# Seventeen small extra loads queued behind the first V load of a single-token attention and ReGLU block

## The chip, the cores and the metric

One Trainium2 chip, one core of it. The metric is the device time of one execution in microseconds (us). The kernel before was timed three times: 1038.66 us in the median, 1038.58 to 1039.75 us in all.

## The reference, cut to what matters

One token goes through an attention block with a long cache and then through a gated feed-forward block, everything in float32:

```
q   = layernorm(x) @ wq                     # 640 -> 32 heads x 192
s   = q . k_cache * 192 ** -0.5             # 8192 keys a head
o   = softmax(s) . v_cache
h   = x + concat(o) @ wo
out = h + (relu(n @ W_gate) * (n @ W_up)) @ W_down    # n = layernorm(h), 640 -> 1536 -> 640
```

The caches hold 32 heads x 8192 positions x 192 numbers each, 201 MB for K and as much for V. Each number is read once and used once, for a single token.

## The kernel before, in words

Everything the core reads is packed on the host into long rows, one row for each of the 128 partitions of SBUF, so that a load is always a block of 128 partitions. For head h, `kk[h]` is the K block (12288 float32 a row, 6144 KB in all) and `vv[h]` the V block (14208 a row, 7104 KB: the V cache of the head, its slice of `wo`, and the `wq` of the next head). The last V block comes from `v0` in two pieces, the `wq` of the first head with the input x from `w0`, and the feed-forward weights lie in `ww`, loaded in six pieces that `CUTS` sets. All of them go into one SBUF tile, `big`: one place for K and two places for V, in turn.

SyncE (SP) issues all of these loads, in the order of its program (`sync_fn`): `w0`, K of head 0, V of head 0, and then a loop over two heads at a time that issues K, V, K, V. K of head i waits for the semaphore `sp`, which TensorE raises when the scores of head i - 1 are done (line 132), since there is a single place for K. V of head i waits for `wo`, raised when the output of an earlier head has been multiplied with its slice of `wo` (line 137). Behind the loop come the last K in two halves, the last V in two pieces, and, after the last scores and outputs (lines 155 and 156), the six pieces of `ww` (line 158). Line 160 stores the result.

For each head TensorE makes the query (`query`, out of the `wq` that came with the V block before), the scores (`scores`, 24 matmuls into the PSUM tile `sp`), and the output (`output`). VectorE takes the maxima and multiplies V with the weights of the softmax (`ttr`, line 126, 12 of them a head, with `columns` in the middle). ScalarE makes the exponentials and the masks. TensorE's matmuls all have line 328, that of a helper. The feed-forward block at the end takes each piece of `ww` as it lands (`weights`, line 399, and `project`): its last matmuls into `pq` need the last two pieces.

GpSimd (POOL) fills constants at the start. At the end it waits for the result (`s_o4`, line 185) and clears the semaphores (line 186). A small load of x (four rows of 160 numbers, line 288) goes out on ScalarE's queue at the start. It is the only load on that queue.

Words used below: a "packet" is one piece of a load that one of the core's 16 DMA engines moves. A "closing write" is the four-byte packet with which an engine reports the end of its part of a load to the load's semaphore; a load raises its semaphore by 16 in all. A "landing" is the moment at which all of a load has been reported.

Of the kernel before, what the change touches and what calls it, by code (L numbers as in the profile page):

```python
# [10 lines left out]
P, Q, NQ = 128, 32, 4  # L11
# [15 lines left out]
JV = 7  # L27
GATE, DOWN, FW = DJ * F, 2 * DJ * F, 2 * DJ * F + FJ * D
CUTS = (0, GATE, GATE + 3 * F, DOWN + 2 * D, DOWN + 8 * D, DOWN + 11 * D, FW)
SCALE = DH ** -0.5  # L30
EPS = 1e-5

# [26 lines left out]
def mha_decode_reglu_kernel(nc, x, w0, kk, vv, v0, ww, out):  # L59
    names = ("xr", "k", "k2", "va", "vb", "vb1", "qd", "qs", "sp", "mp", "pt", "m1", "rs",  # L60
             "pl", "q", "op", "po", "o", "o2", "wo", "cst", "st", "ffn0", "ffn1", "ffn2", "ffn3", "ffn4",
             "ffn5", "h4", "hm", "hc", "hr", "pu", "us", "pg", "gu", "pd", "pool", "dve")
    stored, s_o4 = (nc.alloc_semaphore("e_" + n) for n in ("out", "o4"))
    s = {n: nc.alloc_semaphore("e_" + n) for n in names}
    nums = sorted(x.num for x in s.values())
# [2 lines left out]
    def sb(name, shape):  # L68
        return nc.alloc_sbuf_tensor(name, shape, F32).ap()

    def ps(name, shape):
        return nc.alloc_psum_tensor(name, shape, F32).ap()
# [33 lines left out]
    h4 = sb("h4", [P, DG])  # L106
    hs1 = sb("hs1", [P, 1])
    hT = sb("hT", [P, DJ, Q])
    hc = sb("hc", [P, DJ, Q])
    hsq = sb("hsq", [P, DJ])  # L110
    us = sb("us", [P, FG])
    gu = sb("gu", [P, FG])
    guT = sb("guT", [P, FJ, Q])
    o4 = sb("o4", [P, DG])

    sp = ps("sp", [P, SG])
    pq = ps("pq", [P, QB])
# [7 lines left out]
    def ttr(eng, dst, a, b, scale, res):  # L125
        return eng.tensor_tensor_reduce(out=res, in0=a, in1=b, scale=scale, scalar=0.0,  # L126
                                        op0=ALU.mult, op1=ALU.add, accum_out=dst)

    def sync_fn(sy):
        def load_k(h, n, dst=kt, c=slice(0, KW), sem="k"):  # L130
            if n is not None:
                sy.wait_ge(s["sp"], n)
            sy.dma_start(dst[:, c], kk[h][:, c]).then_inc(s[sem], 16)  # L133

        def load_v(h, n, b):
            if n is not None:
                sy.wait_ge(s["wo"], n)
            sy.dma_start(vts[b], vv[h]).then_inc(s["vb" if b else "va"], 16)

        sy.dma_start(vt2[:, VW + KW + WO:2 * VW + DJ], w0).then_inc(s["vb"], 16)  # L140
        load_k(0, None)
        load_v(0, None, 0)
        sy.sem_inc(s["k2"], 16 * (H - 1))
        sy.sem_inc(s["vb1"], 16 * (H // 2))
        with sy.Fori(1, H - 2, 2) as i:
            load_k(i, i)
            load_v(i, i, 1)
            load_k(i + 1, i + 1)
            load_v(i + 1, i + 1, 0)
        load_k(H - 1, H - 1, c=slice(0, KW // 2))  # L150
        load_k(H - 1, None, c=slice(KW // 2, KW), sem="k2")
        sy.wait_ge(s["wo"], H - 1)
        for c0, c1, n in ((0, JV * SG, "vb"), (JV * SG, KW + WO, "vb1")):
            sy.dma_start(vts[1][:, c0:c1], v0[:, c0:c1]).then_inc(s[n], 16)
        sy.wait_ge(s["wo"], H)
        sy.wait_ge(s["sp"], H)
        for i, (c0, c1) in enumerate(zip(CUTS, CUTS[1:])):
            sy.dma_start(big[:, c0:c1], ww[:, c0:c1]).then_inc(s[f"ffn{i}"], 16)  # L158
        sy.wait_ge(s_o4, 1)
        sy.dma_start(out[0].rearrange("o (g n) -> (o g) n", g=NQ), o4[0:P:Q, :]).then_inc(stored, 16)  # L160

    def pool_fn(g):
        c = Chain(g, s["pool"])
        c(g.memset(ones, 1.0))
        c(g.memset(share, 1.0 / C))
        c(g.memset(eps, EPS))
        c(g.memset(pick, 0.0))
        c(g.memset(op, 0.0))
        c(g.memset(rl, 1.0))
        c(g.memset(vts[1][:, KW:KW + WO], 0.0))  # L170
        c(g.memset(ident, 0.0))
        c(g.memset(quad, 1.0))
        c.sync()
        c(g.affine_select(out=quad, in_=quad, compare_op=ALU.is_ge, fill=0.0, base=0,
                          pattern=[[1, P]], channel_multiplier=-Q))
        c(g.affine_select(out=ident, in_=ident, compare_op=ALU.not_equal, fill=1.0, base=0,
                          pattern=[[-1, P]], channel_multiplier=1))
        for i in range(2):
            c(g.memset(pick[:, i, i, :], 1.0))
        c.sync()  # L180
        c(g.affine_select(out=quad, in_=quad, compare_op=ALU.is_ge, fill=0.0, base=Q - 1,
                          pattern=[[-1, P]], channel_multiplier=Q))
        c.sync()
        g.sem_inc(s["cst"], 1)
        g.wait_ge(s_o4, 1)
        g.sem_clear(range(nums[0], nums[-1] + 1))

    def vector_fn(v):
# [42 lines left out]
        def columns(n):  # L231
            v.wait_ge(s["q"], n)
            ttr(v, q[:, 0:1], ident, pq[:, 0:D1], SCALE, junk[:, 0:D1])
            ttr(v, q[:, 1:2], low, pq[:, D1:DH], SCALE, junk[:, D1:DH]).then_inc(s["qd"])

# [90 lines left out]
    def tensor_fn(t):  # L326
# [72 lines left out]
        def weights(c0, n):  # L399
            if c0 in CUTS:  # L400
                t.wait_ge(s[f"ffn{CUTS.index(c0)}"], 16)
            return big[:, c0:c0 + n]
# [24 lines left out]
    with nc.Block() as block:  # L427
        block.sync(sync_fn)
        block.scalar(scalar_fn)
        block.gpsimd(pool_fn)  # L430
        block.vector(vector_fn)
        block.tensor(tensor_fn)
# [52 lines left out]
```

## Time and profile before

| what | value |
|---|---|
| median of three runs | 1038.66 us |
| the profiled execution | 1039.44 us |
| its span, first to last instruction | 1037.4 us |
| granted TensorE clock, mean of the span | 0.645 |
| bytes moved | 445.96 MB, mean 430 GB/s |
| busy: TensorE, VectorE, ScalarE | 436.5, 525.2, 74.5 us |

The profiled execution took 2.04 us more than its span, and lies 0.78 us above the median, inside the three runs' own range. In the profile's page the rows of 40 slices show how busy an engine was in each fortieth of the span (25.9 us), in tenths. The list of DMA queues gives packets, MB, and the time that their packets took as a share of the 16 engines' span. In the groups by line, "idle before" names what an engine waited for. A window of the trace can be asked for the same rows, and then the slices are fortieths of the window.

### The profile page before, as it was taken

Reading aid. Unit: us, or ns where it says so; the run is one execution under the profiler, and the core shown is the slowest. Engines: PE = TensorE matmul, PEld = TensorE weight load, DVE = VectorE, ACT = ScalarE, POOL = GpSimd, SP = SyncE. Lnnn points to the kernel's source line nnn. Section 1 sums busy time; section 2 is a strip of 40 time slices with the busy share of each in tenths; the row PEclk is TensorE's granted clock in tenths of the full one; section 3 lists DMA queues with packets and bytes.
Section 4 is the critical chain, followed back from the end, with each engine's and each line's share of the span. In section 5 each row is a group of like instructions: output and inputs, shape, how many; then the busy total and the mean of one; then the engine's idle time right before and its main releaser. Section 6 shows DMA issues by size and latency. Waiting matters only on the chain.

```text
span 1037.4 us, 7424 instructions
## 1 busy us (share of the span) xinstructions
PE 436.5 (42%) x2740; PEld 200.4 (19%) x2740; DVE 525.2 (51%) x1162; ACT 74.5 (7%) x174; POOL 2.8 (0%) x18
## 2 busy tenths in 40 slices
PE   4255343254343354443344443443533443533536
PEld 2122121122121121111221111221211221211202
DVE  1644465644555544556544556444656444656472
ACT  1000000000000000000000000000000000000001
POOL 1000000000000000000000000000000000000000
PEclk8666666666656666655666655666656666666667
DMA  9999999999999999999999999999999999999998
GB/s 402 447 425 432 432 424 451 420 428 432 434 449 420 451 428 432 432 422 449 420 432 432 429 449 420 448 434 432 429 422 449 425 432 432 433 440 422 428 433 344
DMA packets 10531, 445.96 MB, mean 430 GB/s; under 512 B 1176, under 2 KB 1184, under 8 KB 1568
## 3 DMA queue, kind: packets, MB, share of 16 engines
q1 hardware_dynamic: 10520, 445.92, 99.6%
q8 instruction: 2, 0.03, 0.0%
q14 instruction: 1, 0.01, 0.0%
q10 hardware_dynamic: 8, 0.00, 0.0%
HBM read 445.91 MB, written 0.00 MB: 430 GB/s over the span
## 4 chain that ended last, share of the span: by engine, by line
DMA 76%; PE 23%; issue 0%; SPq 0%; DVE 0%; ACT 0%
DMA big<-in_kk_dram 72%; PE sp L328 23%; DMA big<-in_ww_dram 3%; SPq L133 0%; SPq L158 0%; PE pq L328 0%; PE acc L328 0%; SPq L140 0%; DVE junk L126 0%; PE po L328 0%; ACT o L324 0%; DVE o L126 0%
## 5 line engine op out<-in xcount | busy, mean ns | idle before, releaser
L126 DVE CUSTOM_DVE_ANT_0 big<-big,p 128x1024 f32<-128x1024 f32 x384 | 444.9, 1220 | 145.3 <-DMA big<-in_vv_dram 144.1
L328 PE MATMUL sp<-big,qs 128*32 128x512 f32 x1536 | 240.9, 792 | 343.7 <-DMA big<-in_kk_dram 339.3
L328 PE MATMUL pq<-big,xn 128*128 128x192 f32 x320 | 112.9, 539 | 153.0 <-DMA big<-in_vv_dram 151.1
L328 PEld LDWEIGHTS sp<-big,qs 128*32 128x32 f32 x1536 | 56.1, 141 | 514.6 <-DMA big<-in_kk_dram 359.9
L126 DVE CUSTOM_DVE_ANT_0 junk<-blk,po,rl 128x8 f32<-128x8 f32 x66 | 11.9, 218 | 266.9 <-PE po L328 266.9
L328 PEld LDWEIGHTS pq<-big,xn 128*128 128x128 f32 x320 | 97.8, 331 | 155.8 <-DMA big<-in_vv_dram 153.7
L302 ACT ACTIVATE o<-side,o 128x64 f32<-128x64 f32 x33 | 11.5, 348 | 480.5 <-DVE o L126 480.5
L297 ACT ACTIVATE qs<-pick,q 128x64 f32<-128x64 f32 x33 | 11.5, 348 | 408.9 <-DVE q L126 408.9
L307 ACT ACTIVATE p<-sp,m 128x1024 f32<-128x1024 f32 x32 | 35.6, 1113 | 47.9 <-DVE m L247 47.9
L245 DVE TENSOR_REDUCE mp<-sp 128x1 f32<-128x1024 f32 x32 | 39.0, 1219 | 0.0
L328 PE MATMUL pl<-rs,share 128*128 128x1 f32 x64 | 16.5, 327 | 51.9 <-ACT p L307 51.9
L249 DVE RECIPROCAL rl<-pl 128x1 f32<-128x1 f32 x32 | 5.4, 169 | 59.0 <-PE pl L328 59.0
L328 PE MATMUL acc<-big,o 128*32 128x160 f32 x528 | 28.8, 316 | 15.3 <-DVE o L126 15.3
L126 DVE DVE_READ_ACCUMULATOR2_ANT op<- 128x1 f32 x384 | 31.4, 82 | 0.0
L328 PEld LDWEIGHTS pl<-rs,share 128*128 128x128 f32 x64 | 13.7, 267 | 58.0 <-ACT p L307 58.0
L328 PE MATMUL po<-op,same 128*128 128x12 f32 x66 | 13.1, 273 | 15.7 <-DVE op L126 15.7
L328 PEld LDWEIGHTS po<-op,same 128*128 128x128 f32 x66 | 10.0, 191 | 42.6 <-issue 26.8
L247 DVE TENSOR_REDUCE m<-pt 128x1 f32<-128x128 f32 x32 | 9.3, 292 | 13.3 <-PE pt L374 13.3
L328 PEld LDWEIGHTS acc<-big,o 128*32 128x32 f32 x528 | 10.6, 108 | 25.8 <-DVE o L126 18.4
L374 PE MATMUL pt<-ident,mp 128*128 128x128 f32 x32 | 10.3, 323 | 8.9 <-DVE mp L245 8.9
L126 DVE CUSTOM_DVE_ANT_0 junk<-ident,pq 128x128 f32<-128x128 f32 x33 | 9.3, 282 | 3.6 <-PE pq L328 3.6
L298 ACT ACTIVATE qs<-pick,q 128x32 f32<-128x32 f32 x33 | 10.1, 306 | 0.0
(76 smaller groups left out, 70.4 us busy)
## 6 DMA issues: line engine op xcount, KB each, us to landing
big<-in_vv_dram SPq DMA_DIRECT2D x31, 7104.0 KB, 38.7
big<-in_kk_dram SPq DMA_DIRECT2D x31, 6144.0 KB, 23.5
big<-in_kk_dram SPq DMA_DIRECT2D x2, 3072.0 KB, 19.7
big<-in_ww_dram SPq DMA_DIRECT2D x1, 3840.0 KB, 20.3
big<-in_v_dram SPq DMA_DIRECT2D x1, 3584.0 KB, 30.4
big<-in_v_dram SPq DMA_DIRECT2D x1, 3040.0 KB, 37.3
big<-in_ww_dram SPq DMA_DIRECT2D x1, 2304.0 KB, 25.5
big<-in_ww_dram SPq DMA_DIRECT2D x1, 2176.0 KB, 30.2
```

The lines of the kernel that those rows point to most:

```text
L126: return eng.tensor_tensor_reduce(out=res, in0=a, in1=b, scale=scale, scalar=0.0, op0=ALU.mult, op1=ALU.add, accum_out=dst)
L245: v.reduce_max(mp, sp, axis=AX.X).then_inc(s["mp"])
L247: v.reduce_max(m1, pt[:, 0:P], axis=AX.X, negate=True).then_inc(s["m1"])
L249: v.reciprocal(rl, pl[:, 0:1])
L297: a.mul(qs[:, 0:2, :], pk[:, 0:2, :], q[:, 0:1])
L298: a.mul(qs[:, 2, :], pk[:, 2, :], q[:, 1:2]).then_inc(s["qs"])
L302: a.mul(o2, side, o[:, 1:2]).then_inc(s["o2"])
L307: a.activation(p, sp, AF.Exp, bias=m1, accum_out=rs).then_inc(s["rs"])
L328: return t.matmul(dst, lhsT, rhs, start=start, stop=stop, **kw)
L374: t.transpose(pt[:, 0:P], mp.to_broadcast([P, P]), ident).then_inc(s["pt"])
```

## The change

The change puts seventeen loads into SP's program, between the issue of V of head 0 and the loop. Fifteen of them take 15, 14, ... down to 1 partitions, from partition 0 up, with 79 down to 65 numbers a row (64 + k numbers for k partitions, 260 to 316 bytes). One takes 2048 numbers (8192 bytes) a row for partitions 0 to 7, and the last one 2048 numbers a row for partitions 0, 32, 64 and 96. They read the first rows of `ww` into a new tile, `extra`, that nothing reads afterwards. A new semaphore, `jk`, counts them; POOL waits for all of them at the very end, ahead of clearing the semaphores. The new tile comes last of the SBUF tiles, and no other load, tile or instruction is moved.

```
+NE = 16
...
-             "ffn5", "h4", "hm", "hc", "hr", "pu", "us", "pg", "gu", "pd", "pool", "dve")
+             "ffn5", "h4", "hm", "hc", "hr", "pu", "us", "pg", "gu", "pd", "pool", "dve", "jk")
...
+    extra = sb("extra", [P, 5376])
...
         load_k(0, None)
         load_v(0, None, 0)
+        for k in range(NE - 1, 0, -1):
+            sy.dma_start(extra[0:k, k * 80:k * 80 + 64 + k], ww[0:k, 0:64 + k]).then_inc(s["jk"], 16)
+        sy.dma_start(extra[0:8, 1280:3328], ww[0:8, 0:2048]).then_inc(s["jk"], 16)
+        sy.dma_start(extra[0:P:Q, 3328:5376], ww[0:P:Q, 0:2048]).then_inc(s["jk"], 16)
         sy.sem_inc(s["k2"], 16 * (H - 1))
...
         g.wait_ge(s_o4, 1)
+        g.wait_ge(s["jk"], 16 * (NE + 1))
         g.sem_clear(range(nums[0], nums[-1] + 1))
```

This is SP's program before, from the first load (`w0`) to the first loads of the loop. The rows marked ISA are the waits for `sp` and `wo`, and each load is named by its target and its source with partitions x numbers:

```order
L140 DMA big<-in_w_dram 128x965
L133 DMA big<-in_kk_dram 128x12288
L138 DMA big<-in_vv_dram 128x14208
L145 UNCONDITIONAL_BRANCH
L133 ISA
L133 DMA big<-in_kk_dram 128x12288
L138 ISA
L138 DMA big<-in_vv_dram 128x14208
```

And this is the same place after the change, from the fourth-last of the shrinking loads on (lines stand four to seven further down, and the eleven wider ones of the kind stand ahead of these rows, behind V of head 0):

```order
L146 DMA extra<-in_ww_dram 4x68
L146 DMA extra<-in_ww_dram 3x67
L146 DMA extra<-in_ww_dram 2x66
L146 DMA extra<-in_ww_dram 1x65
L147 DMA extra<-in_ww_dram 8x2048
L148 DMA extra<-in_ww_dram 4x2048
L151 UNCONDITIONAL_BRANCH
L135 ISA
L135 DMA big<-in_kk_dram 128x12288
```

SP now issues all seventeen ahead of its first wait and of K of head 1. The order of all other rows, on SP and on the other engines, is what it was.

## The prediction

> **What bounds the kernel now.** I began with the profile's page: the DMA row of 40 slices, the list of queues, and the chain that ended last.
>
> ```profile
> DMA  9999999999999999999999999999999999999998
> DMA packets 10531, 445.96 MB, mean 430 GB/s; under 512 B 1176, under 2 KB 1184, under 8 KB 1568
> q1 hardware_dynamic: 10520, 445.92, 99.6%
> q10 hardware_dynamic: 8, 0.00, 0.0%
> DMA 76%; PE 23%; issue 0%; SPq 0%; DVE 0%; ACT 0%
> ```
>
> Queue q1, SP's, keeps the 16 DMA engines busy for 99.6% of the span. Mean 430 GB/s is 26.9 GB/s for each of them. The chain gives TensorE 23%, but that is not a bound: it is the wait of the next K load for the scores, and the engines move V meanwhile. So whatever puts work on a DMA engine makes that engine later, unless it ends early anyway. Nothing here can be sped up by adding loads, except by chance at the two ends.
>
> The packet counts tell how a load is split. There are 73 loads of 128 partitions (1 `w0`, 33 K, 33 V, 6 `ww`). With 128 rows and 16 closing writes each they make 73 x 144 = 10,512 packets, and the store of four rows must make the remaining 8 of q1's 10,520. The load of x, four rows, makes q10's 8. So **four rows make four closing writes**, not 16: a load of four partitions runs on four engines, one of k small partitions on k. Which four, the counts do not say.
>
> Next I asked for windows at the end, because a delay carried by one engine counts only if that engine ends last. Here is the DMA row of the 5 us from 1032.4 on (slices of 0.125 us), from the trace:
>
> ```profile
> DMA  9421303011111110000000000000000000000000
> q1 hardware_dynamic: 80, 0.17, 8.9%
> ```
>
> At 1032.65 a fifth of the engines is still busy, and from 1033.4 to 1034.3 only about a tenth, that is one to three of 16. Most engines are done near 1032.8, and **two or so end 1.5 us behind the crowd**. Why they do, two short windows show (47 to 50 us and 1023 to 1026 us, 3 us each):
>
> ```profile
> q8 instruction: 1, 0.02, 2.1%
> ```
> ```profile
> q8 instruction: 1, 0.02, 2.3%
> ```
>
> In each, a single packet of instructions took 2.1% or 2.3% of 16 x 3 us, 1.0 and 1.1 us of one engine. That engine stays late, since it never idles afterwards. The end of the program hangs on those two:
>
> ```profile
> big<-in_ww_dram SPq DMA_DIRECT2D x1, 960.0 KB, 36.2
> big<-in_ww_dram SPq DMA_DIRECT2D x1, 320.0 KB, 36.5
> ```
> ```profile
> 1034.01 1.29 PE L328 MATMUL pq<-big,guT 128*32 128x160 f32 x32 [0.48 <-DMA big<-in_ww_dram]
> ```
>
> TensorE's last matmuls begin when the last but one weight piece has landed, and 3.4 us later the span is over. A delay of the latest engine moves this whole tail.
>
> **The change part by part.** *Issue.* SP issues 17 more loads ahead of its next wait. Prices of one issue, by line, and the small ones:
>
> ```profile
> L158 SPq DMA_DIRECT2D big<-in_ww_dram x6: 327/432/441, 996.0 to 998.2; - x6
> ```
> ```profile
> L288 ACTq DMA_DIRECT2D xrow<-in_x_dram x1: 558/558/558, 0.8 to 0.8; - x1
> ```
> ```profile
> 1.74 0.43 SPq L138 DMA_DIRECT2D big<-in_vv_dram  x1
> 26.42 0.35 SPq L133 DMA_DIRECT2D big<-in_kk_dram  x1
> ```
> ```profile
> 35.70 1.22 DVE L126 CUSTOM_DVE_ANT_0 big<-big,p 128x1024 f32<-128x1024 f32 x1 [4.86 <-DMA big<-in_vv_dram]
> ```
>
> From V's issue, over at 2.17, 17 x 0.43 = 7.3 us reach 9.5; at the 0.56 of the four-row load it is 11.7. K of head 1 is issued at 26.42, once the scores of head 0 are done, so the issue is hidden behind that wait with some 15 us in hand. V of head 0 lands just ahead of 35.70, and only past that would the engines run dry. To bite at all, an issue would have to take over (35.0 - 2.2) / 17 = 1.9 us. Nothing waits behind SP there but K and V of head 1. A full backlog does not stop SP either: the six `ww` issues, made while a V piece was still moving, took 0.43 each like the others. Cost: nothing.
>
> *Bytes.* The fifteen small loads hold 35,680 bytes, the two others 65,536 and 32,768 (4 rows x 8192), 133,984 in all. Spread evenly that is 0.31 us at 430 GB/s, the least that the engines can pay together. They are not spread evenly: by the counts, k rows go to k engines.
>
> *The heaviest engine.* If the loads always take the same first engines, the first one gets 15 small rows, 2 rows of 8192 bytes and 17 closing writes. A large row costs 8192 / 26.9 = 0.305 us, both 0.61. For a small row the nearest row is the four-row load of x (640 bytes a row). In the window from 1.7 to 1.9 us its queue shows
>
> ```profile
> q10 hardware_dynamic: 8, 0.00, 5.7%
> ```
>
> 5.7% of 16 x 0.2 us is 0.18 us for four rows with their closing writes, 0.046 us a pair. Fifteen pairs are at most 0.68 us by that row, and at least 0.16 us (4,320 bytes at 26.9 GB/s). I take 0.04 a pair, near the row, because fixed costs weigh more than bytes here: 0.6 us. **Sum for the heaviest engine: 0.6 + 0.6 = 1.2 us**, between 0.8 and 1.3. Those with one large row get 0.6 to 0.8, and the rest 0 to 0.3.
>
> [...]
>
> *At the end.* POOL's extra wait is for loads that landed a thousand us before. Cost: nothing; the result's store covers it too.
>
> *The sum.* 1.2 us on the heaviest engine reaches the end whole if a late engine carries the same, and not at all if the two late ones carry none, since 1.2 fits into the 1.5 us by which they trail. Against the profiled 1039.44 that is 1040.6, and against the median, 0.78 lower, 1039.9. About 0.2%, 2.1 us, is what a measurement of this kernel can tell from no change.
>
> **The rivals.** *Hidden.* The late engines are not the carriers, or carry a few small rows: +0 to +0.6, 1038.7 to 1039.3. For it stands the tail, which has room for 1.2 us; against it, that half of the engines carry a large row, so with two late engines chosen at random one mostly does.
>
> *Crowding at the target, the rival that ends slower.* In a full load each engine writes eight partitions of its own at 26.9 GB/s. If that rate belongs to the way into a group of partitions and not to the engine, then eight engines that all write to partitions 0 to 7 take turns. With all eight on one way the neighbouring load takes 65,536 / 26.9 = 2.4 us instead of 0.3, and its engines stand still for that long. Where a late engine is among them, the end moves by 2.4 to 2.8 us, to about 1041.3; where none is, by 2.4 - 1.5 = 0.9 at least. It decides from 2.1 us on. For it: 26.9 is the only rate that any row shows, and no row of before has two engines writing to neighbours. Against it: the four rows of x went in 0.046 us each with closing, not four times their byte time of 0.024.
>
> [...]
>
> *Closing writes that wait for each other.* If each of the 17 closing writes on the first engine waited for the landing before it, 0.2 us apiece would add 3.4 us. K and V in turn show no such stall at 99.6% busy, but there the closing writes are a load apart. Time: 1041 to 1043.
>
> *The change does not do what it says.* If all 16 engines share the rows evenly, it is 0.3 us, within the hidden case. If the longer SP program moves the instruction packets to other engines, the tail could shrink by at most its 1.5 us, to 1037.2, which is still no more than 0.2%.
>
> **How the numbers follow.** Forecast, +0.9 to +1.4 us (the carrier's own cost on a late engine, or crowding without a late carrier): 0.42. Hidden or even, down to a smaller tail: 0.23. Crowding with a late carrier, +1.8 to +2.8: 0.23, some 0.20 of it over 2.1. Waiting closing writes or a stopped issue: 0.12. That gives slower 0.32, within 0.2% 0.66, and 0.02 for a gain that I cannot name. The predicted time is the forecast's, 1039.9. The range from 1038.5 to 1041.4 holds the forecast, the hidden case and crowding to 2.7 us; it leaves out the closing writes, the smaller tail and the top of crowding.
>
> **What would show it.** q1 grows by 132 rows and 132 closing writes to 10,784 packets, and packets under 512 bytes from 1176 to 1428. SP's seventeen issues end before 13 us, and K of head 1 is still issued near 26.4. The steady rate of the middle stays 430 GB/s or so. The tail's slices tell the rest: forecast right, the last busy slice is 1.2 us later while the crowd's is hardly moved; hidden, a broader shoulder with the same last slice; crowding, four to eight engines that trail by 2 us or more. I am wrong if K of head 1 is issued late, if the rate in the middle has changed, or if the time leaves the range.

## The result and the profile after

The changed kernel takes 1041.2 us in the median of 18 runs (1040.42 to 1042.95), the kernel before 1038.94 us in as many (1038.45 to 1040.33). The ratio is 1.002, with a 95% interval of 1.0014 to 1.0027: 2.26 us more. That is small, but the interval lies wholly above 1. The profiled execution took 1040.42 us, with a span of 1038.9 us against 1037.4.

First the page of the changed kernel, with the lines that answer to those of before, and below them the issues of the extra loads and of K of head 1 from its timeline (start, duration, line; K's line is 135 now and was 133):

```profile
DMA  9999999999999999999999999999999999999998
DMA packets 10795, 446.09 MB, mean 429 GB/s; under 512 B 1428, under 2 KB 1436, under 8 KB 1820
q1 hardware_dynamic: 10784, 446.05, 99.6%
q10 hardware_dynamic: 8, 0.00, 0.0%
DMA 76%; PE 23%; issue 0%; SPq 0%; DVE 0%; ACT 0%
```
```profile
2.19 5.65 SPq L146 DMA_DIRECT2D extra<-in_ww_dram  x15
7.88 0.27 SPq L147 DMA_DIRECT2D extra<-in_ww_dram  x1
8.20 0.65 SPq L148 DMA_DIRECT2D extra<-in_ww_dram  x1
26.11 0.39 SPq L135 DMA_DIRECT2D big<-in_kk_dram  x1
```

The counts are as worked out: 264 packets more on q1, 1428 under 512 bytes. The seventeen issues are over at 8.85 us, and K of head 1 is issued at 26.11, a little earlier than before. The engines are as busy as they were, so the time did not go into waiting for a load to be issued. It went into the loads that lie behind the extra ones. Here is the chain of waits around K of head 1 (start, duration), before and after:

```profile
26.42 25.20 DMA big<-in_kk_dram
```
```profile
26.11 27.18 DMA big<-in_kk_dram
```

K of head 1 lands at 53.29 instead of 51.62, 1.7 us later, though it was issued sooner. That delay never goes away: the last piece of K lands at 993.05 us instead of 991.44. At the other end, the DMA row of the same 5 us from 1032.4 on (slices of 0.125 us) and TensorE's last matmuls of the changed kernel:

```profile
DMA  4979989795664454654212111100000000000000
q1 hardware_dynamic: 217, 0.75, 37.1%
```
```profile
1035.55 1.29 PE L335 MATMUL pq<-big,guT 128*32 128x160 f32 x32 [0.46 <-DMA big<-in_ww_dram]
```

Before, the row fell to a fifth at 1032.65 and was empty from 1034.3 on. Now it stays at seven to nine tenths until 1033.5, at about half until 1034.75, and shows nothing from 1035.65 on (one engine of 16 is less than a tenth; the last row ends at 1035.84). So **the whole crowd of engines is about 1 us later**, half of them trail by another microsecond, and the last matmuls begin 1.5 us later.

### The profile page after: what moved, and what is told of

Read it like the earlier page. It is cut to its first block, busy times and chain, and to the rows that moved or that the text cites. A ratio compares the mean times of both kernels' runs of the same rounds, so it can differ in the third digit from the quotient of the medians.

```text
span 1038.9 us, 7442 instructions
## 1 busy us (share of the span) xinstructions
PE 435.2 (42%) x2740; PEld 200.3 (19%) x2740; DVE 525.2 (51%) x1162; ACT 74.5 (7%) x174; POOL 2.8 (0%) x18
## 2 busy tenths in 40 slices
DMA packets 10795, 446.09 MB, mean 429 GB/s; under 512 B 1428, under 2 KB 1436, under 8 KB 1820
## 3 DMA queue, kind: packets, MB, share of 16 engines
q1 hardware_dynamic: 10784, 446.05, 99.6%
## 4 chain that ended last, share of the span: by engine, by line
DMA 76%; PE 23%; issue 0%; SPq 0%; DVE 0%; ACT 0%
DMA big<-in_kk_dram 72%; PE sp L335 23%; DMA big<-in_ww_dram 3%; SPq L135 0%; SPq L164 0%; PE pq L335 0%; PE acc L335 0%; SPq L142 0%; DVE junk L128 0%; PE po L335 0%; ACT o L331 0%; DVE o L128 0%
```

## The experiments

Two theories were on trial: that the extra loads cost each engine only its own packets ("own cost"), and that engines which write to neighbouring partitions take turns at the target ("crowding"). A third suspect, a slow long row behind every extra load, came from the trace after. All kernels compute the whole reference; the extra loads are used by nothing.

**Each part alone.** Of the seventeen loads, the first kernel keeps the fifteen small ones, the second the eight neighbours, the fourth the four distant rows. The third sends the eight rows to every fourth partition:

```
-        sy.dma_start(extra[0:8, 1280:3328], ww[0:8, 0:2048]).then_inc(s["jk"], 16)
+        sy.dma_start(extra[0:32:4, 1280:3328], ww[0:8, 0:2048]).then_inc(s["jk"], 16)
```

> The fifteen shrinking loads alone. Theory 'crowding' (a group of neighbouring partitions has one way of 26.9 GB/s, and on top of it the first long row behind an extra load is slow, 2.4 us instead of 1.8): the small rows cost 0.02 us each with closing, 0.35 us on the heaviest engine; the slow first row adds 0.6 us on the engines that carried one. Span 0 to 1.0 us over that of before, and in the window where K of head 1 begins no row of 8192 bytes. Rival 'own cost' (each packet costs its own engine its bytes and nothing else): 0.35 us on the heaviest engine, no slow first row, span unchanged within the tail's 1.5 us.

> The load of 8192 bytes to partitions 0 to 7 alone. 'Crowding': its eight rows take 0.3 to 1.2 us each (two groups of four that take turns, 32 KB at 26.9 GB/s being 1.2 us), the carriers fall 1.2 to 1.8 us behind, the span grows by 0.3 to 2. 'Own cost': all eight rows take 0.31 us and the span does not move beyond the tail. If the slow first row is a matter of the whole chip and not of the carriers, all 16 engines show it, else eight.

> The same eight rows of 8192 bytes, sent to partitions 0, 4, 8 ... 28 instead of 0 to 7. 'Crowding' at groups of four neighbours: each row has a way of its own, 0.31 us each, the carriers fall 0.3 us behind plus the slow first row. 'Own cost': the same 0.31 us as for neighbours. If the source (the same rows of the weights) and not the target made the rows slow, they take 0.3 to 1.2 us as for the neighbours.

> The load to partitions 0, 32, 64 and 96 alone. [...] 'Own cost': 0.31 us each. Span within 1 us of before by both; the slow first row on four engines, or on all 16 if it is not a matter of the carriers.

One execution each took 1039.92 us (small), 1040.57 (neighbours), 1038.85 (spread) and 1038.97 (distant), beside 1038.77 for the kernel before. The 18 runs of the kernel before lie up to 1.9 us apart, so single times say little. The trace's packets say more. This table is made from them: the first row of K of head 1 (49,152 bytes) on each of the 16 engines, in ns, and the rows of 8192 bytes.

```
kernel            first K row: shortest, median, longest    rows of 8192 bytes
before            1815  1815  1815                          none
all seventeen     2394  2444  3168                          307 to 1587
small alone       1815  2400  3469                          none
neighbours alone  2479  2546  2627                          309 (five), 355, 405, 546
spread alone      1815  1815  1815                          309 (all eight)
distant alone     1927  1960  2284                          309 (all four)
```

Three things follow. The same eight rows from the same source leave the long rows behind them as they were when they go to partitions 0, 4, 8 ... 28, so it is the target that matters. With neighbours **all 16 engines lose 0.7 us** on their next long row, also the eight that carry none of the load; the rows of 8192 bytes themselves mostly show nothing. And a slow long row does not follow every extra load: that third suspect falls. The small loads lengthen this row by up to 1.65 us on some engines and leave it nearly untouched on six (1815 to 1839 ns), which is not the pattern of the neighbours.

The packets say more about the small loads. Each load's rows have a size of their own (316 bytes in the first, 4 fewer in each next one), so the sizes tell how many of the fifteen an engine took part in: one engine in all fifteen, one in fourteen, and so on down to one in none. This is how much later the engine ends its first row of K than the engines of before did, counted from its last row of V (eight of the 16 engines are shown; the others lie between them, thirteen at 1.81 and fourteen at 1.68):

| small loads on the engine | 0 | 4 | 5 | 6 | 7 | 8 | 12 | 15 |
|---|---|---|---|---|---|---|---|---|
| later, us | 0.02 | 0.09 | 0.14 | 0.28 | 0.54 | 0.97 | 1.48 | 1.98 |

A small row and its closing write take 0.022 us of the engine in the record. Up to four loads cost just that. **From the sixth on the price rises**, and eight or more come to 0.12 to 0.14 us a load. With all seventeen loads the same engine, the one with all fifteen small rows and two large ones, loses 3.05 us: 0.33 in the small rows, 2.1 in the two large rows (1587 and 528 ns) and 0.6 in the row of K.

The neighbours' price can be seen in the rate too. These windows go from 34 to 38 us; the last two columns are the DMA share and GB/s. First the kernel before, then the spread, then the neighbours:

```profile
34.00:38.00 4.00, 2.27 (x7) 2.27 (x8) 2.29 (x3) 0.00 (x0) 0.00 (x0) 0.50 0.91 393
```
```profile
34.00:38.00 4.00, 2.21 (x7) 2.22 (x8) 2.23 (x3) 0.00 (x0) 0.00 (x0) 0.50 0.95 410
```
```profile
34.00:38.00 4.00, 1.38 (x4) 1.38 (x5) 1.40 (x3) 0.00 (x0) 0.00 (x0) 0.50 1.03 360
```

Two long rows fill such a window, so it counts coarsely, and the GB/s have to be read by the share: 393 / 0.91 and 410 / 0.95 are both 432, and 360 / 1.03 is 350.

**One load behind every V.** A microsecond or two is near the noise, so the next kernels issue a load 31 times, once behind each V of a head. SP waits for the one before first. That takes up to 9.6 us (with the neighbours), but the next K is issued some 20 us later, so it holds up nothing:

```
         load_v(0, None, 0)
+        sy.dma_start(extra[0:8, 0:2048], ww[0:8, 0:2048]).then_inc(s["jk"], 16)
...
             load_v(i, i, 1)
+            sy.wait_ge(s["jk"], i * 16)
+            sy.dma_start(extra[0:8, 0:2048], ww[0:8, 0:2048]).then_inc(s["jk"], 16)
...
             load_v(i + 1, i + 1, 0)
+            sy.wait_ge(s["jk"], i * 16 + 16)
+            sy.dma_start(extra[0:8, 0:2048], ww[0:8, 0:2048]).then_inc(s["jk"], 16)
```

The others differ only in the load: `extra[0:32:4, 0:2048]` (spread), `extra[0:P:Q, 0:2048]` from `ww[0:P:Q, 0:2048]` (distant), `extra[:, 0:64]` from `ww[:, 0:64]` (128 small rows), `extra[0:1, 0:64]` from `ww[0:1, 0:64]` (one small row).

> One load of 8192 bytes to partitions 0 to 7 behind each V of a head, 31 in all, to make the price of one readable in the time. 'Crowding': four rows of 8192 bytes at 26.9 GB/s are 1.2 us on each of two ways, and with a slow first row 1.8 us, so 31 of them add 37 to 56 us. 'Own cost': 31 x 0.31 = 10 us less the tail, +8 us; own cost and slow first row together, 31 x 0.9 = +28 us.

> The same 31 loads, sent to partitions 0, 4, 8 ... 28. 'Crowding': no turns to take, so 31 x 0.31 us plus a slow first row of 0.6 us each, +28 us, 10 to 28 us less than with the neighbours. 'Own cost': +8 us, and the same as with the neighbours.

> One load of 64 numbers (256 bytes) for all 128 partitions behind each V, 31 in all: eight small rows on each engine, no two engines on one target. By bytes and packets 8 x 0.02 us each, 31 x 0.17 = +5 us. With a slow first row behind each, 31 x 0.77 = +24 us. Crowding plays no part here, so this separates the slow row from it.

> One row of 256 bytes to partition 0 behind each V, 31 in all: one small packet and one closing write on a single engine. By bytes and packets 31 x 0.02 = +0.7 us, hidden in the tail. If a slow first row follows each on that engine, 31 x 0.6 = 19 us less the tail, +17 to +19 us.

> The load of four rows of 8192 bytes to partitions 0, 32, 64 and 96 behind each V, 31 in all. With a way of its own for each row it costs as the spread load of eight did, 31 x 0.31 = +9 us. [...]

| load behind each V | time, us | ratio to before, 95% | more, us | by 31, us |
|---|---|---|---|---|
| eight neighbours | 1086.96 | 1.0457 [1.0427, 1.0487] | 48.1 | 1.55 |
| eight spread by four | 1048.19 | 1.0084 [1.0055, 1.0113] | 9.3 | 0.30 |
| four: 0, 32, 64, 96 | 1060.75 | 1.021 [1.0166, 1.0254] | 21.8 | 0.70 |
| 128 small rows | 1043.72 | 1.0042 [1.0022, 1.0061] | 4.9 | 0.16 |
| one small row | 1039.56 | 1.0004 [0.9993, 1.0016] | 0.7 | 0.02 |

The first four stand beside 1038.86 us for the kernel before, the distant rows (third line) beside 1038.93. **Crowding is shown**: the same 64 KB from the same rows cost 0.30 us a load when spread, as one row of 8192 bytes does by its bytes, and 1.55 us at neighbours. That the rows take turns, four on a way, is argued from the size: four by their bytes are 1.2 us, eight on one way would be 2.4. The rows' own records do not show the turns, and what makes up the other 0.35 us is not known; behind the single load the eight carriers lost 1.0 to 1.3 us each. Four distant rows, half the bytes, cost 0.70, more than twice the spread load. That fits two pairs that share a way, at 0.61 us a pair by bytes (2 x 8192 / 26.9, an estimate); whether rows pair up, and which, this run does not show. 128 small rows cost their packets, 8 x 0.02 us, and the lone row nothing that can be measured; both misses of the slow row theory.

Windows from 66 to 958 us show that the price is paid all along, at a rate that is lower in the middle and not at the ends (last column, GB/s): before, then spread, then neighbours.

```profile
66.00:958.00 892.00, 369.71 (x2222) 170.70 (x2222) 464.79 (x1005) 59.72 (x142) 0.00 (x0) 0.63 1.00 433
```
```profile
66.00:958.00 892.00, 369.01 (x2222) 170.78 (x2222) 456.35 (x987) 59.17 (x140) 0.00 (x0) 0.63 1.00 432
```
```profile
66.00:958.00 892.00, 353.28 (x2133) 161.78 (x2133) 436.17 (x945) 57.05 (x135) 0.00 (x0) 0.62 0.99 416
```

With neighbours the engines are still 99% busy, at 416 GB/s: the larger part of the loss lies inside the packets' own durations. Over the whole execution the neighbours' queue shows

```profile
q1 hardware_dynamic: 11016, 447.95, 98.0%
```

of a span of 1085.7 us, 1064 us of packets on the mean engine. Before it was 99.6% of 1037.4, 1033 us. So about 31 of the 48 us are packets, the extra rows and longer long ones, and the rest is time in which an engine stood idle. An engine that lost less must wait for the others at the latest when the next K is due, since K is issued only after all of the last one has landed; that this is what the idle time consists of was not tested.

**Several small loads in a row.** Crowding was also my explanation of the fifteen small loads, so three kernels issue eight of them (15 down to 8 partitions) behind each V: to neighbours as in the change, to every eighth partition, and to neighbours with rows cut to 256 bytes at multiples of 256:

```
+            sy.wait_ge(s["jk"], i * 128)
+            for k in range(15, 7, -1):
+                sy.dma_start(extra[0:k, k * 80:k * 80 + 64 + k], ww[0:k, 0:64 + k]).then_inc(s["jk"], 16)
...
-                sy.dma_start(extra[0:k, k * 80:k * 80 + 64 + k], ww[0:k, 0:64 + k]).then_inc(s["jk"], 16)
+                sy.dma_start(extra[0:8 * k:8, k * 80:k * 80 + 64 + k], ww[0:k, 0:64 + k]).then_inc(s["jk"], 16)
...
-                sy.dma_start(extra[0:k, k * 80:k * 80 + 64 + k], ww[0:k, 0:64 + k]).then_inc(s["jk"], 16)
+                sy.dma_start(extra[0:k, k * 64:k * 64 + 64], ww[0:k, 0:64]).then_inc(s["jk"], 16)
```

> Eight of the shrinking loads (15 down to 8 partitions, rows of 288 to 316 bytes, partitions from 0 up) behind each V, 31 times. Own cost alone: 8 x 0.022 = 0.18 us a head on the heaviest engine, +4 us. Crowding by bytes: partitions 0 to 3 take 32 rows, 9.7 KB, 0.36 us a head, +10 us. Crowding by rows, at the 0.04 us a row that the fifteen loads alone seemed to cost on their way: 1.2 us a head, +35 us.

> The same loads with the same rows, bytes and columns, sent to every eighth partition (0, 8, 16 ...) instead of neighbours. If neighbours are what makes small rows dear, this costs little more than the packets, +4 to +10 us, and clearly less than the neighbours. If the short rows at odd addresses are dear by themselves, it costs the same as the neighbours.

> The same loads to neighbours, each row cut to 256 bytes and put at a multiple of 256 bytes. If the odd sizes and addresses make small rows dear, this costs a third to a half of the neighbours' price, near the bytes' +9 us; if each row on a way costs the same whatever its address, it costs what the neighbours cost.

They took 1070.49, 1071.61 and 1071.83 us beside 1038.93 (ratios 1.0304 [1.0259, 1.0348], 1.0315 [1.027, 1.0359] and 1.0317 [1.0272, 1.0361]): 31.6, 32.7 and 32.9 us more, 1.02 to 1.06 us a head. **Crowding falls for the small loads**, and so do odd sizes and addresses: neither the wider spacing nor the alignment lowers the price. It is also near what the engine with eight small loads lost when the fifteen ran alone, 0.97 us. The kernel with 128 small rows is the counterpart: there each engine also gets eight small rows a head, in one load with one closing write, and pays 0.16 us. Eight rows in eight loads cost 1.02 to 1.06. So rows and bytes are not what is dear. What differs is the number of loads that follow one another on an engine, eight against one, 0.13 us each on the average of eight. Two things go with it and stay untested apart: the closing writes, and the target, since row j of each of the eight loads goes to the same partition while the 128 rows go to one partition each. The queues tell the two apart at a glance (packets, MB, share); the 128 rows first, then the eight loads:

```profile
q1 hardware_dynamic: 14984, 446.93, 99.7%
```
```profile
q1 hardware_dynamic: 16224, 446.79, 99.1%
```

Nearly the same bytes and a similar number of packets, 27 us apart. In the windows from 66 to 958 us these two run at

```profile
66.00:958.00 892.00, 370.56 (x2222) 170.84 (x2222) 460.32 (x997) 59.72 (x142) 0.00 (x0) 0.63 1.00 432
```
```profile
66.00:958.00 892.00, 356.59 (x2147) 164.53 (x2151) 450.35 (x973) 57.61 (x137) 0.00 (x0) 0.63 1.00 422
```

432 and 422 GB/s, with full engines in both. Whether the closing writes wait for each other, each load's start costs something on the engine, or rows to the same partition are slow, these runs do not separate; I call it the price of loads in a row. No experiment came out ahead of the kernel before, so there is no better version to run.

## Why the prediction was right or wrong, step by step

The range of 1038.5 to 1041.4 holds the measured 1041.2, near its top, because it was drawn wide enough for a rival (crowding to 2.7 us). The predicted 1039.9 had a rise of 1.2 us, and 2.26 was measured. The forecast's own path, a late engine that carries 1.2 us more, is not what happened: the heaviest engine lost 3.05 us, and the tail hid half of it.

*The bound, the issue and the packet counts* came out as argued. The issue of all seventeen took 6.6 us, and K of head 1 was not late.

*The heaviest engine, small rows.* This step failed in size. I took 0.04 us a pair and at most 0.046, from the four rows of x. The small rows themselves are recorded with 0.02 us, even less. But the price shows up in the row behind them: with the fifteen alone the worst engine loses 1.65 us there, and 15 x 0.022 us before it, 2.0 us in all or 0.13 a load on average. The row of x could not tell: each of its engines carries a single small row. So the term was 2.0 us and not 0.6. That the loads always take the same first engines, which the sum assumed and no view of before showed, the packets of after bear out: the engines with eight or more small rows are those that carry the large ones. "Closing writes that wait for each other" was nearest, a price that comes with the number of loads, at 0.13 us on average instead of the 0.2 that I tried. But a fixed price for each load does not fit the engines with up to five, which lost next to nothing; whether the closing writes are the cause stays open.

*The heaviest engine, large rows.* 0.305 us a row is right where each row has a target of its own (0.309 in the trace, 0.30 by the time). It fails for neighbours and for the distant rows: among all seventeen the two on the heaviest engine took 2.1 us and not 0.61, with the price of the small loads before them in it. "Crowding at the target" named the rival that the target decides, and 1.2 us for four rows that take turns, an estimate by bytes, is the better part of the measured 1.55. It did not foresee that engines without any of the rows lose 0.7 us too. The rival's text held that no row of before has two engines writing to neighbours. The load of x does, to partitions 0 to 3, and its four rows took 29, 29, 42 and 46 ns, too short to tell.

*The tail.* I let the 1.5 us of the late engines hide what the carriers lose, and this was wrong for crowding: its price falls on all 16 engines, also those that carry nothing. The trace's packets can be followed row by row to each engine's last row. Before, thirteen engines ended between 1032.43 and 1032.92 us, one at 1033.52, and at 1034.29 and 1034.32 the two that had carried the packets of instructions. After, six engines without a large row end between 1033.43 and 1033.59, 1 us later: the delay that all engines share reached the end. The two with the packets of instructions end at 1034.87 and 1035.10. The last three, at 1035.14, 1035.63 and 1035.84, each carry two large rows. So the last engine is now a carrier and not one of the two late ones, and it ends 1.5 us after the last of before: about 1 is the crowd's shift, and 0.5 what the carriers trail further than the late engines did. That these 1.5 us lie near the forecast's 1.2 is luck. The heaviest engine's loss was put 1.8 us too low, and the room in the tail, which the forecast did not count on, took about 1.5 us away. Why the median rose by 0.7 us more than the profiled pair is not settled: the profiled execution before lies above its median, the one after is the fastest of its 18.

*The chances.* Within 0.2% had 0.66, slower by more 0.32. The measured ratio of 1.002 lies on the line between them, its interval on both sides.

## What to carry to other kernels

In this stream of loads, which kept the DMA engines 99.6% busy in the kernel before, the bytes of an extra load were 0.30 us of its 1.55 at neighbours. Keep large rows off neighbouring partitions (every fourth one cost only its bytes here, 0.30 us), and make one load of several: eight rows for each engine cost 0.16 us in one load and 1.02 to 1.06 us in eight. A few small loads in a row, up to four on an engine here, cost no more than their records show (0.09 us for four). Read the price of more in the packets behind the small ones and in the rate of the stretch, since the small packets' own records do not show it.

## What the hardware showed that I had not expected

A load of 64 KB to eight neighbouring partitions slows all 16 engines for a moment, not only the eight that carry it: the next row of 49,152 bytes takes 2.48 to 2.63 us on each engine instead of 1.815. And a small packet can look cheap in its own record (0.02 us, its closing write 0.009) while a run of eight to fifteen loads of them costs 0.12 to 0.14 us a load on the engine, paid by the long row that follows; a run of up to five costs next to nothing more (0.14 us for five, of which the records hold 0.11).

The late engines at the end come from packets of instructions: in the kernel before, two engines carried one such packet each, of 1.0 and 1.1 us, at 48 and 1024 us, and stayed late. They trail by 1.5 us and not 1.0 because here, too, the next row pays: the one behind the first packet took 2.28 us where such rows take 1.82, and the one behind the second 1.12 where they take 0.65.
